# Spreading a weight conversion over three passes and moving low parts to GpSimd

## The chip, the cores and the metric

The kernel runs on one core of a Trainium2 chip. The metric is device time in microseconds (us) of one execution. Engines are named as in the profile: PE is TensorE's matmul, PEld its weight load, DVE is VectorE, ACT ScalarE, POOL GpSimd, SP the engine whose queue issues all the DMAs.

## The reference

A retention layer is followed by two feed-forward layers on 2304 tokens of width 512, all kept in float32:

```
ret = (q @ k^T * scale * decay) @ v              # 4 batches x 8 heads, 576 x 64
x   = (silu(x @ w_gate) * (x @ w_val)) @ w_out   # layer 1, inner width 1536
x   = (max(x @ w_in, 0) ** 2) @ w_out            # layer 2, inner width 2048
```

The activations are float32; the weights of both layers are float64.

## The kernel before, in words

**Stages.** Retention comes first. Then come five passes: (1, 0) and (1, 1) for layer 1, (2, 0), (2, 1) and (2, 2) for layer 2. A pass takes two blocks of tokens (512 each in layer 1, 384 in layer 2) through all "systems" of its layer: a system is 256 inner columns of one weight matrix ("g" gate, "v" value, "i" layer 2's input). There are 12 systems in a pass of layer 1 and 8 in one of layer 2. Pass (1, 0) carries a further 256 tokens, the plain chunk ("c").

**Products.** A system is done as a 2 x 2 block product with seven multiplications instead of eight: `slot(n, i)` does multiplication i of system n into PSUM (`g`, `v`, `z`) and its combinations on ACT and DVE (`cag`, `cav`, `cbg`, `cbv`, 128x512 per row). Each operand is split into a high part (ACT's copy to float32r) and a low part (source minus high, DVE), and PE does three matmuls per product. `hidden` (L678) splits the activated columns: "a" and "b" for the two token blocks, "c" for the plain chunk, into `ho_hi` and `ho_lo`. The second matmul (`out1`, `out2`) adds `oacc` into the resident `xy` on DVE.

**Weights.** A unit is one tile of 64-bit weights: layer 1 has 36 units, layer 2 has 32. `words` (L150) converts a unit in two ACT and four DVE instructions: the clamp (TENSOR_SCALAR on 128x512 f32), a shift and mask (TENSOR_SCALAR on uint32), SCALAR_TENSOR_TENSOR, and a last sum, which the profile calls CUSTOM_DVE_ANT_0 and the order ISA. All write `w`. Two `raw` buffers hold loaded words. Layer 1's results stay in SBUF, at most `HOLD` = 5 at a time; layer 2's are stored in DRAM (`wst`) and loaded again as `w_in` or `wo`. In a layer's first pass POOL forms the combinations of a weight tile (`s`, `w`, `w_in`), ACT and DVE split them into `wi`, and `wi` and `wo` are stored (`win`, `wsp`) for the later passes.

**Order.** The loop at the end emits, for each step n, ten entries of `seq` (slots of system n and n - 1, and the thirds 0, 1, 2 of the output tiles). After each slot it advances the build of the next system's weights and the conversion by `PACE` parts (five parts are a unit). `ensure` (L245) forces a conversion that is needed and not there. A scheduler with its own timeline then orders each engine's queue by when it expects the operands, so that a queue's order is not the emitted order. Each engine works off its queue in order: what stands behind a waiting instruction waits too.

Of the kernel before, what the change touches and what calls it, by code (L numbers as in the profile page):

```python
# [9 lines left out]
F32 = mybir.dt.float32  # L10
F32R = mybir.dt.float32r
U16 = mybir.dt.uint16
U32 = mybir.dt.uint32
AF = mybir.ActivationFunctionType
ALU = mybir.AluOpType
# [6 lines left out]
P = 128  # L22
# [6 lines left out]
M1 = 512  # L29
# [14 lines left out]
UNITS_EARLY = 7  # L44
HOLD = 5

PACE = {(1, 0): 1.3, (1, 1): 1.3, (2, 0): 1.3}

CUT = 256

# [1 line left out]
TINY = float(np.uint32(0x38000000).view(np.float32))  # L52
HUGE = float(np.uint32(0x47F00000).view(np.float32))
# [3 lines left out]
def retention_moe_kernel(  # L57
# [13 lines left out]
    def pool(stack, name, bufs, **kw):  # L71
        return stack.enter_context(
            tc.tile_pool(name=name, bufs=bufs, reuse_waits="tile", **kw)
        )

    keep = pool(ctx, "keep", 1)
    mid = ExitStack()
    ctx.enter_context(mid)
    raw_p = pool(mid, "raw_p", 2)
    cv_p = pool(mid, "cv_p", 1)  # L80
    wb_p = pool(mid, "wb_p", 2)
    part_p = pool(ctx, "part_p", 1, space=bass.MemoryType.DRAM)
    ps_g = pool(ctx, "ps_g", 1, space=PSUM)
# [4 lines left out]
    def f32(ap):  # L88
        return ap.bitcast(F32)
# [3 lines left out]
    class Chained:  # L93


        def __init__(self, engine):
            self.engine, self.last = engine, None

        def __getattr__(self, name):
            op = getattr(self.engine, name)  # L100

            def traced(*args, **kw):
                with ExitStack() as behind:
                    if self.last is not None:
                        behind.enter_context(tc.issue_after(self.last))
                    i = op(*args, **kw)  # L106
                if chain["on"]:
                    self.last = i.ins
                return i

            return traced

    pe, dve, act, pool_e, sp = map(Chained, (nc.tensor, nc.vector, nc.scalar, nc.gpsimd, nc.sync))


    order = [(1, what, f) for k in range(F1 // 2) for what in "gvo" for f in (2 * k, 2 * k + 1)]
    order += [(2, what, f) for k in range(F2 // 2) for what in "io" for f in (2 * k, 2 * k + 1)]
    raw_t, raw_flat, w_t = {}, {}, {}
    spare, ready = [], {}
    loads = {"next": 0, "raw": 0, "open": False, "cap": len(order) - 1, "held": 0}  # L120

    def prefetch(upto):

# [21 lines left out]
    def finish(i):  # L145
        if i in w_t:
            sp.dma_start(out=wst[order[i]], in_=w_t.pop(i).bitcast(F32))
            stored.add(order[i])

    def words(raw, back, flat):  # L150

        ts = dve.tensor_scalar
        both = raw.rearrange("p a (n two) -> p a n two", two=2)
        low, high = both[:, :, :, 0], both[:, :, :, 1]
        low16 = raw.bitcast(U16).rearrange("p a (n four) -> p a n four", four=4)[:, :, :, 1]
        wt = cv_p.tile([P, 512], U32, tag="w", name="w", bufs=HOLD + 1)
        w = wt.rearrange("p (a n) -> p a n", a=2)
        wf = w.bitcast(F32)
        act.activation(out=low, in_=low16, func=AF.Copy, scale=2.0**-13)
        act.activation(out=wf, in_=high.bitcast(F32), func=AF.Abs)  # L160
        yield wt
        ts(out=wf, in0=wf, scalar1=TINY, scalar2=HUGE, op0=ALU.max, op1=ALU.min)
        yield wt
        yield wt
        ts(out=w, in0=w, scalar1=3, scalar2=0x3FFFFFFF, op0=ALU.logical_shift_left, op1=ALU.bitwise_and)
        yield wt
        dve.scalar_tensor_tensor(
            out=w, in0=high, scalar=0xC0000000, in1=w, op0=ALU.bitwise_and, op1=ALU.bitwise_or
        )
        yield wt  # L170
        if back is None:
            adds = [(wt, flat.rearrange("p (n two) -> p n two", two=2)[:, :, 0])]
        else:
            adds = [(w[:, a], low[:, a]) for a in range(2)]
        for to, lo in adds:
            dve.tensor_tensor(out=to, in0=to, in1=lo, op=ALU.add)
# [28 lines left out]
    def catch_up():  # L205
        while behind:
            lo, src, hi = behind.pop(0)
            dve.tensor_tensor(out=lo, in0=src, in1=hi, op=ALU.subtract)

    def split(hi, lo, src):  # L210
        act.copy(hi, src)
        behind.append((lo, src, f32(hi)))
        if not chain["on"]:
            catch_up()
# [51 lines left out]
    def three(dst, a, b, first, last):  # L266
# [5 lines left out]
    tt = dve.tensor_tensor  # L272
# [3 lines left out]
    systems = [  # L276
        (ph, p, k, what)
        for ph, p in passes
        for k in range((F1, F2)[ph - 1] // 2)
        for what in ("gv", "i")[ph - 1]  # L280
    ]
# [26 lines left out]
        split(*xo[i], src)  # L308

    def temp(tag, rows):  # L310
        return c4_p.tile([P, rows, M1], F32, tag=tag, name=f"c{tag}", bufs=1 + (tag[1] == "g"))

    built = {}
    inputs = {}
# [267 lines left out]
    c4_p = pool(ctx, "c4_p", 1, side="right")  # L582
# [93 lines left out]
    hid = {}  # L676

    def hidden(n, which, c):  # L678
        hi = ho_p.tile(list(c.shape), F32R, tag=f"h{which}", name="ho_hi")
        lo = ho_p.tile(list(c.shape), F32R, tag=f"l{which}", name="ho_lo")  # L680
        split(hi, lo, c)
        hid[n, which] = hi, lo

    wos = {}
# [3 lines left out]
    def load_out(n, fs):  # L688
        ph, p = systems[n][:2]
        for f in fs:  # L690
            key = (ph, "o", f)
            w = wos[f] = wo_p.tile([P, 2, 512], F32R, tag="wo", name="wo")
            if p:
                sp.dma_start(out=w.bitcast(F32), in_=wsp[key])
                continue
            if ph == 1:
                ensure(key, ready)
                src = ready.pop(key)
                loads["held"] -= 1
                act.copy(w[:, 0], src)  # L700
                pool_e.tensor_tensor(out=w[:, 1], in0=src, in1=f32(w[:, 0]), op=ALU.subtract)
            else:
                ensure(key, stored)
                sp.dma_start(out=w[:, 1].bitcast(F32), in_=wst[key])
                act.copy(w[:, 0], f32(w[:, 1]))
                tt(out=w[:, 1], in0=f32(w[:, 1]), in1=f32(w[:, 0]), op=ALU.subtract)
            sp.dma_start(out=wsp[key], in_=w.bitcast(F32))

    turn["o"] = 0
# [38 lines left out]
    flip = systems.index((2, 0, 0, "i"))  # L748
# [12 lines left out]
    def after(n, i):  # L761
# [4 lines left out]
        if i in (1, 2, 3, 4, 5, 7):  # L766
            for j in (5, 6) if i == 5 else (i,):
                renew(passes[passes.index(at) + 1], j)

    ho_p = pool(mid, "ho_p", 1)  # L770
    gate_p = pool(mid, "gate_p", 1)
    wo_p = pool(mid, "wo_p", 4)
    pace = {"due": 0.0}
    pumped["limit"] = 10 ** 6
    end = len(systems)
    for n in range(end + 4):
        ph, p, k, what = systems[n] if n < end else (0, None, 0, "")
        tiles = outs.get(n, [])
        cuts = [len(tiles) * x // 3 for x in range(4)] if n != flip + 1 else [0] + 3 * [len(tiles)]
        seq = [(1, n), (7, n - 1), 0, (2, n), (4, n - 1), 1, (6, n), (3, n - 1), 2, (5, n)]  # L780
        if (ph, p) == (1, 0):
            seq.insert(5, (("s", 0), n))
            seq.append((("s", 1), n))
        if n == 0:
            for x in range(4):
                sp.dma_start(out=later[x][0], in_=later[x][1])
            later.clear()
            load_in(1)
            renew((1, 0), 4)
            renew((1, 0), 3)  # L790
        make = build(n + 1) if n + 1 < end else iter(())
        if n + 2 < end and systems[n + 2][1] == 0:
            load_in(n + 2)
        for x in fetch.get(n, []):
            load_out(*x)
        for x in seq:
            if x in (0, 1, 2):
                for fn, *args in tiles[cuts[x]:cuts[x + 1]]:
                    fn(*args)
                continue  # L800
            i, k = x
            if n == flip + 1 and i == 4:
                mid.close()
                ho_p = pool(ctx, "ho2_p", 3)
                wo_p = pool(ctx, "wo2_p", 8)
            if not 0 <= k < end:
                continue
            if isinstance(i, tuple):
                plain_slot(k, i[1])
            else:  # L810
                slot(k, i)
            next(make, None)
            if n < flip - 1:
                pace["due"] += PACE[ph, p]
                pump(int(pace["due"]))
                pace["due"] %= 1
            after(k, i)
        for _ in make:
            pass
        if n == flip - 1:  # L820
            for _ in convert:
                pass

# [60 lines left out]
```

## Time and profile before

| | us |
|---|---|
| median of 3 runs | 903.7 (901.61 to 904.12) |
| the profiled execution | 903.78 |
| its span | 902.0 |
| PE busy | 876.7 |
| DVE busy | 649.2 |
| ACT busy | 397.4 |
| POOL busy | 120.5 |

The span runs from the first to the last instruction; 1.8 us of the profiled execution lie around it. Retention fills the first 98 us; the passes end near 336, 519, 645 and 770 us.

### The profile page before, as it was taken

To read this page: it belongs to the slowest core of one execution; us is meant where nothing else is said; L and a number is where in the kernel's file an instruction comes from. 1 tells how busy PE (TensorE), PEld (TensorE's weight loads), DVE (VectorE), ACT (ScalarE), POOL (GpSimd) and SP (SyncE) were. 2 spreads that over 40 slices of the span, in tenths; PEclk is the share of its full clock that TensorE was granted. 3 is DMA by queue.
4 is the path that set the end of the run, shared out by engine and by line. 5 is a ranking of instruction groups with operands and counts; after the bars stand their busy time and mean duration, and the time that the engine had idled before them with its cause. 6 is when DMAs were issued, how large, how long until landed. Compare 5 with 4: busy or idle time off the path is not lost.

```text
span 902.0 us, 13463 instructions
## 1 busy us (share of the span) xinstructions
PE 876.7 (97%) x5050; PEld 747.6 (83%) x5050; DVE 649.2 (72%) x1019; ACT 397.4 (44%) x708; POOL 120.5 (13%) x131
## 2 busy tenths in 40 slices
PE   8898999999999999999999999999999999999997
PEld 6786778788877778877888889899989889889886
DVE  3889997989898898777747898768543467534443
ACT  2566676654545554544423546544223233233210
POOL 2351522512221110000001231300000000000000
PEclk9999999999999999999999999999999999999999
DMA  9985676656567879889654459855774575666402
GB/s 327 353 297 197 237 265 206 206 206 220 180 216 248 274 276 292 293 291 305 246 180 140 173 205 399 305 188 201 245 243 157 171 224 187 189 219 219 144 34 71
DMA packets 73041, 203.61 MB, mean 226 GB/s; under 512 B 7440, under 2 KB 18192, under 8 KB 72976
## 3 DMA queue, kind: packets, MB, share of 16 engines
q1 hardware_dynamic: 72976, 202.75, 65.7%
q8 instruction: 40, 0.66, 0.3%
q14 instruction: 25, 0.20, 0.1%
HBM read 138.23 MB, written 64.49 MB: 225 GB/s over the span
## 4 chain that ended last, share of the span: by engine, by line
PE 66%; DVE 15%; DMA 11%; issue 4%; ACT 3%; SPq 1%; POOL 1%; ACTq 0%; DVEq 0%; POOLq 0%
PE oacc L106 32%; PE g L106 17%; PE v L106 9%; DMA raw<-in_w 8%; DVE w L106 6%; PE z L106 4%; DVE xy L106 2%; PE o L106 2%; PE s L106 1%; DVE wi L106 1%; ACT w L106 1%; DVE xo_l L106 1%; ACT raw L106 1%; DMA kv_sb<-in_kv 1%; DMA qk_sb<-in_qk 1%
## 5 line engine op out<-in xcount | busy, mean ns | idle before, releaser
L106 PE MATMUL g<-xo_h,wi 128*128 128x384 f32 (+1 forms) x768 | 242.3, 366 | 3.2 <-ACT cbv L106 1.3
L106 PE MATMUL oacc<-wo,ho_hi 128*128 128x512 f32 x576 | 182.4, 392 | 0.2 <-ACT wo L106 0.2
L106 PEld LDWEIGHTS g<-xo_h,wi 128*128 128x128 f32 x768 | 142.4, 188 | 24.5 <-ACT cbv L106 2.9
L106 PE MATMUL oacc<-ho_hi,wo 128*128 128x512 f32 (+1 forms) x480 | 152.1, 372 | 5.1 <-DVE xy L106 3.7
L106 PE MATMUL g<-xo_l,wi 128*128 128x384 f32 (+1 forms) x384 | 139.7, 364 | 0.0
L106 DVE TENSOR_TENSOR xy<-oacc,xy 128x512 f32<-128x512 f32 (+1 forms) x154 | 99.3, 651 | 47.9 <-PE oacc L106 47.5
L106 PE MATMUL v<-xo_h,wi 128*128 128x512 f32 (+1 forms) x384 | 124.7, 365 | 0.1
L106 PEld LDWEIGHTS oacc<-wo,ho_hi 128*128 128x128 f32 x576 | 107.2, 188 | 19.1 <-ACT wo L106 0.6
L106 PE MATMUL oacc<-wo,ho_lo 128*128 128x512 f32 x288 | 113.4, 394 | 0.0
L106 PEld LDWEIGHTS oacc<-ho_hi,wo 128*128 128x128 f32 x480 | 87.9, 188 | 24.1 <-DVE xy L106 5.5
L106 ACT ACTIVATE raw<-raw 128x512 uint32<-128x512 uint16 x68 | 46.0, 677 | 124.8 <-DMA raw<-in_w 112.5
L106 DVE TENSOR_SCALAR w<-w 128x512 f32<-128x512 f32 (+1 forms) x136 | 65.4, 481 | 34.5 <-ACT w L106 33.5
L106 PE MATMUL oacc<-ho_lo,wo 128*128 128x512 f32 (+1 forms) x240 | 89.2, 372 | 0.6 <-DVE ho_lo L106 0.6
L106 DVE TENSOR_TENSOR cbg<-v,cbg 128x384 f32<-128x384 f32 (+1 forms) x72 | 43.0, 598 | 54.1 <-ACT cbg L106 39.7
L106 PEld LDWEIGHTS g<-xo_l,wi 128*128 128x128 f32 x384 | 72.1, 188 | 9.0
L106 PEld LDWEIGHTS v<-xo_h,wi 128*128 128x128 f32 x384 | 71.3, 188 | 9.1 <-DVE cbg L106 0.5
L106 PE MATMUL v<-xo_l,wi 128*128 128x512 f32 (+1 forms) x192 | 69.9, 364 | 0.0
L106 PE MATMUL z<-xo_h,wi 128*128 128x512 f32 (+1 forms) x192 | 62.4, 366 | 1.7 <-DVE cav L106 1.7
L106 PEld LDWEIGHTS oacc<-wo,ho_lo 128*128 128x128 f32 x288 | 54.0, 188 | 11.0
L106 ACT ACTIVATE cag<-g 128x384 f32<-128x384 f32 (+1 forms) x36 | 18.9, 525 | 89.6 <-PE g L106 89.5
L106 ACT CAST ho_hi<-cbg 128x768 fp32r<-128x768 f32 (+1 forms) x36 | 32.6, 906 | 51.5 <-DVE cbg L106 51.5
L106 ACT COPY cbg<-g 128x384 f32<-128x384 f32 (+1 forms) x72 | 37.0, 514 | 39.3 <-PE g L106 39.1
(84 smaller groups left out, 1310.8 us busy)
## 6 DMA issues: line engine op xcount, KB each, us to landing
wi<-win SPq DMA_DIRECT2D x84, 512.0 KB, 4.0
raw<-in_w SPq DMA_DIRECT2D x68, 512.0 KB, 4.4
win<-wi SPq DMA_DIRECT2D x60, 512.0 KB, 3.7
wo<-wsp SPq DMA_DIRECT2D x44, 512.0 KB, 6.0
wsp<-wo SPq DMA_DIRECT2D x28, 512.0 KB, 5.9
qk_sb<-in_qk SPq DMA_DIRECT2D x15, 576.0 KB, 6.9
kv_sb<-in_kv SPq DMA_DIRECT2D x15, 576.0 KB, 6.2
wst<-w SPq DMA_DIRECT2D x32, 256.0 KB, 4.7
```

Of the source, the lines that this page charges most:

```text
L106: i = op(*args, **kw)
```

## The change

- Layer 2's conversion is emitted in all three passes (1, 0), (1, 1) and (2, 0), by new numbers in `PACE` (parts per slot in the first systems of a pass, how many, and parts after that). The buffers `raw_p` and `cv_p` therefore live to the end; half of the `w` buffers (`cv2_p`) and layer 1's intermediates (`c4m_p`) are freed at the switch to layer 2.
- The clamp may not be queued on DVE ahead of the instruction that was the last one two slots earlier (`place`).
- In pass (1, 0), `hidden` computes the low parts of "b" and "c" on POOL instead of DVE. `load_out` does so for layer 2's `wo`.
- In layer 2, "a" has two buffers of `ho_hi` and `ho_lo`, and in steps with "a" tiles the two last of the three tiles come before slot 4 of the system before.

```diff
-PACE = {(1, 0): 1.3, (1, 1): 1.3, (2, 0): 1.3}
+PACE = {(1, 0): (10, 1.5, 1.2), (1, 1): (8, 1.5, 0.1), (2, 0): (8, 1.0, 1.0)}
...
-        wt = cv_p.tile([P, 512], U32, tag="w", name="w", bufs=HOLD + 1)
+        loads["turn"] += 1
+        wt = (cv_p if late2["on"] or loads["turn"] % 2 else cv2_p).tile([P, 512], U32, tag="w", name="w")
...
-        ts(out=wf, in0=wf, scalar1=TINY, scalar2=HUGE, op0=ALU.max, op1=ALU.min)
+        with ExitStack() as held:
+            if place:
+                held.enter_context(tc.issue_after(place[0]))
+            ts(out=wf, in0=wf, scalar1=TINY, scalar2=HUGE, op0=ALU.max, op1=ALU.min)
...
-        split(hi, lo, c)
+        if systems[n][:2] == (1, 0) and which != "a":
+            act.copy(hi, c)
+            pool_e.tensor_tensor(out=lo, in0=c, in1=f32(hi), op=ALU.subtract)
+        else:
+            split(hi, lo, c)
...
-                tt(out=w[:, 1], in0=f32(w[:, 1]), in1=f32(w[:, 0]), op=ALU.subtract)
+                pool_e.tensor_tensor(out=w[:, 1], in0=f32(w[:, 1]), in1=f32(w[:, 0]), op=ALU.subtract)
...
+        if n > flip + 1 and tiles and tiles[0][2] == "a":
+            seq[4:6] = seq[5], seq[4]
+            cuts[2] = 3
...
-            if n < flip - 1:
-                pace["due"] += PACE[ph, p]
+            place[:] = place[1:] + [dve.recent]
+            if (ph, p) in PACE:
+                first, early, later_ = PACE[ph, p]
+                pace["due"] += early if n - systems.index((ph, p, 0, ("gv", "i")[ph - 1][0])) < first else later_
...
-        if n == flip - 1:
+        if (ph, p) == (2, 0) and systems[n + 1][1]:
```

The moves below are at three places. The first is POOL's queue early in pass (1, 0), where `w` and `s` are the weight combinations. Before:

```order
L106 TENSOR_TENSOR s_1503<-w 128x256
L106 TENSOR_TENSOR w<-w 128x256
L106 TENSOR_TENSOR w<-s_1503,w 128x256
L106 TENSOR_TENSOR w<-w 128x256
L106 TENSOR_TENSOR s_1641<-w 128x256
L106 TENSOR_TENSOR w<-w 128x256
L106 TENSOR_TENSOR w<-s_1641,w 128x256
L106 TENSOR_TENSOR w<-w 128x256
L106 TENSOR_TENSOR wo<-w,wo 128x512 x2
L106 TENSOR_TENSOR s_1794<-w 128x256
```

And now, at the same place:

```order
L107 TENSOR_TENSOR ho_lo<-gate,ho_hi 128x512
L107 TENSOR_TENSOR wo<-w,wo 128x512
L107 TENSOR_TENSOR s_1647<-w 128x256
L107 TENSOR_TENSOR w<-w 128x256
L107 TENSOR_TENSOR w<-s_1647,w 128x256
L107 TENSOR_TENSOR w<-w 128x256
L107 TENSOR_TENSOR ho_lo<-cbg,ho_hi 128x1024
L107 TENSOR_TENSOR wo<-w,wo 128x512
L107 TENSOR_TENSOR s_1800<-w 128x256
```

The two low parts of a pair of systems now stand between the weight combinations. The second place is DVE's queue near the end of pass (2, 0), where the weights of its last system are split (`wi` from `w_in` and `s1`). Before:

```order
L106 TENSOR_TENSOR xy_72<-oacc_5892,xy_72 128x4x128
L106 TENSOR_TENSOR ho_lo_5887<-cag_5695,ho_hi_5886 128x768
L106 TENSOR_TENSOR cbg_5696<-v_5814,cbg_5696 128x384
L106 SCALAR_TENSOR_TENSOR cbg_5696<-cbg_5696 128x2x384
L106 TENSOR_TENSOR wi_5929<-w_in_5670,wi_5929 128x512
L106 TENSOR_TENSOR ho_lo_5925<-cbg_5696,ho_hi_5924 128x768
L106 TENSOR_TENSOR xy_72<-oacc_5932,xy_72 128x4x128
L106 TENSOR_TENSOR wi_6023<-s1_5984,wi_6023 128x256
```

Now, from the conversion of that system's second tile (`w_5803`, which becomes `w_in_5790`) on:

```order
L107 ISA w_5803<-raw_5791,w_5803 128x1024
L107 TENSOR_SCALAR w_5814<-w_5814 128x512 x2
L107 SCALAR_TENSOR_TENSOR cag_5822<-g_5821,cag_5822 128x384
L107 SCALAR_TENSOR_TENSOR w_5814<-raw_5801,w_5814 128x512
L107 TENSOR_TENSOR cbg_5823<-v_5950,cbg_5823 128x384
L107 ISA w_5814<-raw_5801,w_5814 128x1024
L107 TENSOR_TENSOR ho_lo_6041<-cag_5822,ho_hi_6040 128x768
L107 SCALAR_TENSOR_TENSOR cbg_5823<-cbg_5823 128x2x384
L107 TENSOR_TENSOR xy_75<-oacc_6086,xy_75 128x4x128
L107 TENSOR_TENSOR ho_lo_6079<-cbg_5823,ho_hi_6078 128x768
L107 TENSOR_TENSOR wi_5991<-w_in_5789,wi_5991 128x512
```

Conversions now stand among the products' combinations there, and the last system's tiles are converted a few instructions before its weights are built. The third place is SP's queue for the same weights. Before:

```order
L106 DMA w_in_5822<-wst_101 128x512
L106 DMA wo_5954<-wst_91 128x512
L106 DMA wo_5959<-wst_92 128x512
L106 DMA wo_5964<-wst_95 128x512
L106 DMA wo_5969<-wst_96 128x512
L106 DMA win_174<-wi_5797 128x1024
L106 DMA w_in_5823<-wst_102 128x512
```

Now:

```order
L107 DMA w_in_5789<-wst_104 128x512
L107 DMA raw_5812<-in_w2 128x1024
L107 DMA wst_105<-w_5803 128x512
L107 DMA wst_106<-w_5814 128x512
L107 DMA wi_6118<-win_156 128x1024
L107 DMA wsp_1373<-wo_6241 128x1024
L107 DMA wsp_1374<-wo_6246 128x1024
L107 DMA w_in_5790<-wst_105 128x512
```

The store and the load of `wst_105` are four queue entries apart; before, the stores of all `wst` lay in the earlier passes.

## Rows read from the trace of the kernel before

**Rows 1.** The page's first line.

```profile
span 902.0 us, 13463 instructions
```

**Rows 2.** By pass: stretch, length, busy PE, PEld, DVE, ACT, POOL, clock, DMA.

```profile
98.00:336.00 238.00, 228.11 (x1149) 189.28 (x1148) 217.93 (x352) 135.92 (x242) 55.52 (x54) 1.00 0.68 232
336.00:519.00 183.00, 181.43 (x806) 147.75 (x805) 137.23 (x215) 81.37 (x131) 9.38 (x10) 1.00 0.71 237
519.00:645.00 126.00, 125.76 (x628) 113.03 (x627) 97.06 (x143) 58.94 (x103) 19.06 (x20) 1.00 0.72 262
645.00:770.00 125.00, 125.00 (x624) 112.47 (x624) 64.83 (x93) 37.55 (x61) 0.00 (x0) 1.00 0.62 198
770.00:902.00 132.00, 127.45 (x624) 112.88 (x622) 56.49 (x81) 28.87 (x48) 0.00 (x0) 1.00 0.44 143
```

**Rows 3.** The same view of parts of passes (1, 0) and (2, 0).

```profile
98.00:198.00 100.00, 93.62 (x477) 77.68 (x476) 92.23 (x149) 62.69 (x117) 29.85 (x30) 1.00 0.68 231
198.00:258.00 60.00, 60.00 (x308) 50.82 (x307) 55.27 (x89) 32.00 (x58) 17.46 (x18) 1.00 0.58 199
258.00:336.00 78.00, 74.49 (x367) 60.77 (x366) 70.43 (x116) 41.23 (x67) 8.20 (x7) 1.00 0.76 260
...
519.00:552.00 33.00, 32.76 (x164) 29.28 (x163) 30.91 (x49) 16.82 (x32) 7.67 (x8) 1.00 0.73 262
```

**Rows 4.** PEld's waits, 98 to 336: total us, times, longest; first and last.

```profile
PEld oacc L106 <- DVE xy L106: 5.5, 7, 1.8
...
PEld v L106 <- DVE cbg L106: 0.3, 1, 0.3
```

**Rows 5.** PEld's waits, 336 to 519, first and last.

```profile
PEld g L106 <- ACT cbv L106: 1.8, 3, 1.2
...
PEld oacc L106 <- ACT ho_hi L106: 0.2, 1, 0.2
```

**Rows 6.** DVE's groups by shape, 98 to 336: busy, mean ns, idle before.

```profile
L106 DVE SCALAR_TENSOR_TENSOR w<-raw,w 128x512 uint32<-128x512 uint32 x39 | 32.0, 821 | 0.4
L106 DVE CUSTOM_DVE_ANT_0 w<-raw,w 128x1024 uint16<-128x1024 uint16 x39 | 29.9, 765 | 0.3
...
L106 DVE TENSOR_TENSOR xy<-oacc,xy 128x512 f32<-128x512 f32 x32 | 21.6, 681 | 0.0
L106 DVE TENSOR_SCALAR w<-w 128x512 uint32<-128x512 uint32 x40 | 20.9, 523 | 0.6
L106 DVE TENSOR_SCALAR w<-w 128x512 f32<-128x512 f32 x40 | 18.4, 461 | 12.1 <-ACT w L106 12.1
...
L106 DVE TENSOR_TENSOR ho_lo<-cbg,ho_hi 128x1024 fp32r<-128x1024 f32 x5 | 6.3, 1263 | 1.0 <-ACT ho_hi L106 1.0
L106 DVE TENSOR_TENSOR ho_lo<-gate,ho_hi 128x512 fp32r<-128x512 f32 x6 | 5.5, 909 | 1.1 <-ACT ho_hi L106 0.9
```

**Rows 7.** The same groups, 336 to 519.

```profile
L106 DVE TENSOR_TENSOR xy<-oacc,xy 128x512 f32<-128x512 f32 x40 | 27.1, 684 | 3.0 <-PE oacc L106 2.8
L106 DVE CUSTOM_DVE_ANT_0 w<-raw,w 128x1024 uint16<-128x1024 uint16 x22 | 15.1, 687 | 0.3
L106 DVE SCALAR_TENSOR_TENSOR w<-raw,w 128x512 uint32<-128x512 uint32 x21 | 14.4, 687 | 0.3
L106 DVE TENSOR_SCALAR w<-w 128x512 f32<-128x512 f32 x20 | 8.5, 426 | 17.5 <-ACT w L106 17.5
...
L106 DVE TENSOR_SCALAR w<-w 128x512 uint32<-128x512 uint32 x20 | 8.4, 422 | 0.3
```

**Rows 8.** DVE's group for layer 2's output weights, 519 to 645.

```profile
L106 DVE TENSOR_TENSOR wo<-wo 128x512 fp32r<-128x512 f32 x16 | 10.6, 685 | 3.2 <-ACT wo L106 3.0
```

**Rows 9.** A low part on POOL, 98 to 336.

```profile
L106 POOL TENSOR_TENSOR wo<-w,wo 128x512 fp32r<-128x512 f32 x10 | 14.5, 1457 | 35.8 <-ACT wo L106 35.8
```

**Rows 10.** DMA issues: count, KB each, median us to landing.

```profile
wst<-w SPq DMA_DIRECT2D x32, 256.0 KB, 4.7
...
w_in<-wst SPq DMA_DIRECT2D x16, 256.0 KB, 5.8
```

More of the change, by code (lines that the diff above doesn't have):

```diff
@@ L76, in retention_moe_kernel @@
     keep = pool(ctx, "keep", 1)
+    raw_p = pool(ctx, "raw_p", 2)
+    cv_p = pool(ctx, "cv_p", 3)
     mid = ExitStack()
     ctx.enter_context(mid)
-    raw_p = pool(mid, "raw_p", 2)
-    cv_p = pool(mid, "cv_p", 1)
+    cv2_p = pool(mid, "cv2_p", HOLD - 2)
     wb_p = pool(mid, "wb_p", 2)
@@ L96, in __init__ @@
         def __init__(self, engine):
-            self.engine, self.last = engine, None
+            self.engine, self.last, self.recent = engine, None, None
         def __getattr__(self, name):
@@ L106, in traced @@
                     i = op(*args, **kw)
+                self.recent = i.ins
                 if chain["on"]:
@@ L119, in retention_moe_kernel @@
     spare, ready = [], {}
-    loads = {"next": 0, "raw": 0, "open": False, "cap": len(order) - 1, "held": 0}
+    loads = {"next": 0, "raw": 0, "open": False, "cap": len(order) - 1, "held": 0, "turn": 0}
+    late2 = {"on": False}
     def prefetch(upto):
@@ L148, in finish @@
             stored.add(order[i])
+    place = []
     def words(raw, back, flat):
@@ L310, in temp @@
     def temp(tag, rows):
-        return c4_p.tile([P, rows, M1], F32, tag=tag, name=f"c{tag}", bufs=1 + (tag[1] == "g"))
+        return (c4_p if tag[1] == "g" else c4m_p).tile([P, rows, M1], F32, tag=tag, name=f"c{tag}", bufs=1 + (tag[1] == "g"))
     built = {}
@@ L678, in hidden @@
     def hidden(n, which, c):
-        hi = ho_p.tile(list(c.shape), F32R, tag=f"h{which}", name="ho_hi")
-        lo = ho_p.tile(list(c.shape), F32R, tag=f"l{which}", name="ho_lo")
-        split(hi, lo, c)
+        kw = dict(bufs=2) if late2["on"] and which == "a" else {}
+        hi = ho_p.tile(list(c.shape), F32R, tag=f"h{which}", name="ho_hi", **kw)
+        lo = ho_p.tile(list(c.shape), F32R, tag=f"l{which}", name="ho_lo", **kw)
+        if systems[n][:2] == (1, 0) and which != "a":
[3 more added lines that the diff above has]
+            split(hi, lo, c)
         hid[n, which] = hi, lo
@@ L768, in after @@
                 renew(passes[passes.index(at) + 1], j)
+    c4m_p = pool(mid, "c4m_p", 1)
     ho_p = pool(mid, "ho_p", 1)
@@ L773, in retention_moe_kernel @@
     pace = {"due": 0.0}
+    place[:] = [dve.last, dve.last]
     pumped["limit"] = 10 ** 6
@@ L803, in retention_moe_kernel @@
                 mid.close()
+                late2["on"] = True
                 ho_p = pool(ctx, "ho2_p", 3)
```

## Prediction

> **What bounds the kernel now.** I read the page's first line [rows 1], then the busy time of every engine by pass, then who PEld waited for, pass by pass. In rows 2 PE is the bound of each pass after retention: 228.1 of 238 us in (1, 0), 181.4 of 183 in (1, 1), 125.8 of 126 in (2, 0), 125.0 of 125 in (2, 1); the 4.6 us in the last row are the end of the kernel. The clock is 1.00 in each row. The matmuls are the same after the change, so it can only win back waits of PE. A PE end is modelled, and a short wait hides in it; PEld, which leads PE, shows more. Its twelve rows in (1, 0), of which rows 4 give the first and the last, add up to 16.4 us, and its nine rows in (1, 1) [rows 5] to 5.5. In (2, 0) PE lost 0.24 us. So some 22 us can be won at most, three quarters of them in (1, 0), where DVE is busy 217.9 of 238 us. Most of those waits are for DVE or ACT results that free a PSUM bank, such as `xy` [rows 4]: DVE works in order, and what frees the bank stands behind a conversion.
>
> DVE's load alone doesn't decide. Rows 3 split the pass: from 198 to 258 DVE is 92% busy and PE loses nothing; from 98 to 198 it is 92% too and PE loses 6.4 us. In (2, 0), from 519 to 552, DVE is 94% busy and PE loses 0.24 us. A wait comes where several DVE instructions that PE doesn't need are queued together, or DVE stands for ACT (12.1 us before the clamp, rows 6).
>
> **Pass (1, 0).** DVE converts 39 units there now [rows 6], 32 after the change, and 22 [rows 7], then 18, in (1, 1); 11 go to (2, 0). The new counts are from the order, between the same combinations. A unit costs DVE 0.821 + 0.765 + 0.523 + 0.461 = 2.57 us in (1, 0) [rows 6], so 7 units are 18.0 us. Twelve low parts leave DVE: six of 128x1024 at 1.263 and six of 128x512 at 0.909 [rows 6], 13.0 us. They become POOL's: 128x512 takes 1.457 us there [rows 9], 128x1024 twice that as an estimate, so 6 x 1.457 + 6 x 2.914 = 26.2 us of POOL.
>
> POOL's work isn't free for DVE. The four conversion rows are slower in (1, 0), with 55.5 us of POOL, than in (1, 1), with 9.4 [rows 2, 6, 7]: 39 x (0.821 - 0.687) + 39 x (0.765 - 0.687) + 40 x (0.523 - 0.422) + 40 x (0.461 - 0.426) = 13.7 us. That is 0.25 us of DVE per us of POOL, and these rows are under half of DVE's work in the pass, so 0.25 is the lower bound; the upper one is 1.0, when DVE stands for the whole POOL instruction. I take 0.35, near the bound that is measured. The 26.2 us then cost DVE 9.2 us, and of the 13.0 us only 3.8 remain. `xy<-oacc`, which reads PSUM, takes 681 ns in one pass and 684 in the other: it pays nothing.
>
> The Trainium skill (SBUF — State Buffer, "Who interferes with whom") says that a VectorE instruction with two SBUF inputs contends with a GpSimd instruction that reads SBUF, and that the later one fully blocks. The trace agrees on which rows pay; by full blocking in every case the 26.2 us would cost DVE 26.2 us and the move of the low parts would be a loss of 13.2.
>
> DVE after: 217.9 - 18.0 - 13.0 + 9.2 = 196.1 us, 0.86 of PE's 228.1 instead of 0.955. What that is worth I bound by two readings. Load: waits were 5.5 us of 183 (3.0%) at 137.2/181.4 = 0.76 and 16.4 of 238 (6.9%) at 0.955; between them 0.86 gives 5.0%, 11.9 us, a gain of 4.5. Bunches: with six units in each pair of systems, where the order before has up to eight, the whole pass could go like 198 to 258 in rows 3, a gain of 16.4. I take 10, the middle. Nothing becomes late on POOL: at 55.5 + 26.2 of 238 us it has room, and `out1` reads these low parts one to two systems (20 to 40 us) later. The POOL row shows what now waits behind a low part: `wo` and the next `s`, both needed a system later.
>
> **Pass (1, 1).** Four units at 0.687 + 0.687 + 0.426 + 0.422 = 2.22 us [rows 7] are 8.9 us of DVE. The longest of the 5.5 us of waits are for ACT's copies, not DVE's [rows 5], so I take 1.5 of them, with 0 and 5.5 as ends.
>
> **Pass (2, 0).** This is what the change pays. DVE gets 11 x 2.22 = 24.4 us of conversion and loses the 10.6 us of `wo` low parts [rows 8], which become 16 x 1.457 = 23.3 us of POOL and cost DVE 0.35 x 23.3 = 8.2. From 97.1 [rows 2] it goes to 119.1 us, 0.947 of PE's 125.8. By load that is like (1, 0) before: 6.7% of 126 us, 8.4 us of waits. By the stretch 519 to 552 [rows 3] it is none. I take the middle, 4.2.
>
> Part of it is a chain with new links. A unit of the last systems now goes through store and reload while the pass runs. From the last sum on `w_5803` to the `wi` that is split from `s1` there are about twenty DVE instructions, some 15 us (an estimate by 0.42 to 0.69 us for a conversion's parts and other 128x512 rows, more for 128x768). The chain needs 4.7 us for the store and 5.8 for the load [rows 10], about 1.5 for the combination on POOL and the split on ACT (an estimate from half of rows 9 and from rows 6), and up to 2.9 more because the load stands in SP's queue behind two `wsp` stores that wait for POOL's low parts (two at 1.457). That is 12.0 to 14.9 us, so the cover is just used up in the last two systems, and in the systems before those it is over 30 us by the same count. Before, all units were stored a pass earlier.
>
> **Costs of nothing.** The place of the clamp adds no instruction; it only lets the products' combinations pass a clamp that waits for ACT. The changed seat of two "a" tiles hands PE the same matmuls; the copy of the next `ho_hi` may now wait for the last tile, but it is needed two systems, 31 us, later, and in (2, 1) DVE is busy 64.8 of 125 us [rows 2]. If that cover fails, it costs a wait of some 0.7 us (one DVE row) in each of twelve steps. Pools that live longer add no instruction. The raw loads, 11 x 512 KB, and their stores go into a pass whose DMA share is 0.72 [rows 2]; in (1, 0), with 0.76 from 258 to 336 [rows 3], loads landed in time for PE, so I give this no price of its own.
>
> **Sum.** -10 - 1.5 + 4.2 = -7.3 us against the profiled execution: its span of 902.0 [rows 1] with 1.8 us around it is 903.8, the same as the median of 903.7. The forecast is **896.5 us**, and its own range, with (1, 0) between -4.5 and -16.4 but not both passes at the same extreme, 890 to 901.
>
> **Rivals.**
> - *No waits at all* (chance 0.10). All of (1, 0) goes like 198 to 258, and (2, 0) like 519 to 552: -16.4 - 1.5 + 0 gives 886. For it: both stretches are over 92% busy. Against: each is short, with few or no conversions in a bunch.
> - *Moved, not removed* (0.22). The waits follow DVE's load: -4.5 in (1, 0), -1.5 in (1, 1), +8.4 in (2, 0) give +2.4; with half of this in doubt, 901 to 906. For it: the load in (2, 0) ends where that of (1, 0) began. Against: rows 3.
> - *POOL stops DVE* (0.16), the slower side. POOL's instructions cost DVE more than 0.35 us each us, since DVE in (2, 0) has little else than rows with two SBUF inputs to do. Without POOL's new work DVE has 97.1 - 10.6 + 24.4 = 110.9 us there, so it passes PE's 125.8 us from a price of 14.9/23.3 = 0.64. At 1.0 it is 134.2 us: +8.4 us, and the reload's chain, with no slack on DVE, adds its 2.9 us. In (1, 0) DVE would have 217.9 - 31.0 + 26.2 = 213.1 us, nearly what it had, a gain of some 2. Together +9: about 912; at 0.7 about 906. For it: the slowed rows. Against: 0.25 measured. The rule of the Trainium skill above (SBUF — State Buffer, "Who interferes with whom") is this case; its full blocking would hold for every instruction, which the measured 0.25 doesn't bear out.
>
> **How the numbers follow.** The forecast has 0.52. The three runs lie within 0.3% of each other, and 0.3% (2.7 us) is about what can be told from no change here. Faster by more, under 901.0: the forecast's 0.52, *no waits* 0.10 and a small part of *moved*, 0.03: 0.65. Slower by more, over 906.4: most of *POOL stops DVE* and the edge of *moved*: 0.15. The rest, 0.20, is the same. The range of 8 in 10 reaches from half of the way to *no waits* to the middle of *moved* and a little further: 889 to 906.
>
> **What would show it.** PEld's waits from 98 to 336 should fall from 16.4 to about 6, and the pass should end some 10 us earlier, with DVE's busy time near 196 and POOL's near 82. `cbg` and `gate` low parts on POOL should take 2.9 and 1.46 us. Pass (2, 0) should be 4 us longer, with DVE near 119 us and waits for `xy`, `wi` or `w`. (2, 1), (2, 2) and the end should take what they took. It is wrong if (2, 0) takes over 135 us (POOL or the reload), if (1, 0) keeps more than 12 us of waits (load decides), or if PE waits for POOL's `ho_lo`.

## The result, and the profile after

The changed kernel takes 909.5 us (median of 6 runs, 907.94 to 910.01), the kernel before 904.0 (901.61 to 905.52) beside it. The ratio is 1.0058 [1.0042, 1.0074]: 5.5 us slower, where 7.2 faster was forecast. The profiled execution took 909.41 us, 1.8 of it around its span:

```profile
span 907.6 us, 13454 instructions
```

The same windows as [rows 2] (length, busy PE, PEld, DVE, ACT, POOL with counts, clock, DMA share, GB/s), of the kernel after:

```profile
98.00:336.00 238.00, 226.33 (x1138) 188.16 (x1138) 201.53 (x310) 128.35 (x227) 74.72 (x65) 0.99 0.58 201
...
519.00:645.00 126.00, 123.82 (x610) 110.79 (x609) 119.82 (x167) 67.49 (x121) 45.06 (x36) 0.99 0.91 325
```

DVE's load moved as meant: 217.9 to 201.5 us in the first window, 97.1 to 119.8 in the third. PE didn't gain by it: it is busy 226.3 us in the first window instead of 228.1. A fixed window holds less work of a slower kernel, so here is the same view by the work, from the first matmul into `z` of (1, 0) to that of (1, 1), before and after:

```profile
88.20:313.10 224.90, 215.25 (x1105) 179.83 (x1104) 205.41 (x331) 132.47 (x241) 59.15 (x55) 1.00 0.65 223
88.30:318.80 230.50, 218.94 (x1123) 183.17 (x1123) 192.70 (x298) 129.46 (x232) 76.70 (x66) 0.99 0.58 202
```

DVE is 12.7 us lighter there, 0.88 of PE's busy time instead of 0.95. PEld's waits in the first fixed window, against the 16.4 us in twelve rows of [rows 4], are in fewer rows and come to 17.9 us:

```profile
PEld oacc L107 <- DVE xy L107: 6.7, 6, 1.9
PEld g L107 <- ACT cbg L107: 4.8, 3, 2.4
PEld oacc L107 <- ACT xy L107: 2.6, 3, 1.2
PEld oacc L107 <- DVE gate L107: 2.0, 2, 1.3
PEld g L107 <- ACT cag L107: 1.3, 1, 1.3
PEld g L107 <- DVE xo_l L107: 0.5, 1, 0.5
```

In (1, 1) the waits fell from 4.9 us to 3.4. (The 5.5 of the prediction hold 0.6 us of waiting for `wo` that belong to (2, 0); the eight rows from 336 to 519, whose first and last are [rows 5], make 4.9.) In (2, 0) they rose from 0.6 to 3.5, most of it in one wait.

DVE's groups of 98 to 336, which answer to [rows 6] (busy, mean ns, idle before):

```profile
L107 DVE SCALAR_TENSOR_TENSOR w<-raw,w 128x512 uint32<-128x512 uint32 x33 | 28.0, 852 | 0.5
L107 DVE CUSTOM_DVE_ANT_0 w<-raw,w 128x1024 uint16<-128x1024 uint16 x32 | 26.4, 826 | 0.2
L107 DVE TENSOR_TENSOR xy<-oacc,xy 128x512 f32<-128x512 f32 x32 | 21.2, 678 | 0.0
L107 DVE TENSOR_SCALAR w<-w 128x512 f32<-128x512 f32 x33 | 18.5, 560 | 9.6 <-ACT w L107 9.6
L107 DVE TENSOR_SCALAR w<-w 128x512 uint32<-128x512 uint32 x33 | 18.3, 558 | 0.4
```

and the low parts on POOL in the same stretch, which [rows 9] stood for:

```profile
L107 POOL TENSOR_TENSOR ho_lo<-cbg,ho_hi 128x1024 fp32r<-128x1024 f32 x5 | 13.4, 2681 | 8.3 <-ACT ho_hi L107 8.3
L107 POOL TENSOR_TENSOR ho_lo<-gate,ho_hi 128x512 fp32r<-128x512 f32 x6 | 9.0, 1499 | 1.5 <-ACT ho_hi L107 1.5
```

Fewer units are converted (32 or 33 instead of 39), but each costs DVE 0.852 + 0.826 + 0.560 + 0.558 = 2.80 us instead of 2.57. Of these rows only `xy<-oacc`, with one input in PSUM, kept its duration (678 ns). The others are longer only where POOL worked beside them. Sorted so over the trace, 25 of the 33 SCALAR_TENSOR_TENSOR rows overlap no POOL instruction and take 0.674 to 0.694 us each; the 8 that overlap one take 1.37 on average. Of the TENSOR_SCALAR rows, 46 alone take 0.42 us and 20 beside POOL 0.88. `xy<-oacc` takes 0.678 us in both cases.

**One wait followed back.** The timeline of the kernel after around PE's longest wait in the pass (start, us, then in brackets the idle time before and what ended it):

```profile
167.61 1.40 DVE L107 TENSOR_SCALAR w<-w 128x512 uint32<-128x512 uint32 x1
168.69 2.58 POOL L107 TENSOR_TENSOR ho_lo<-cbg,ho_hi 128x1024 fp32r<-128x1024 f32 x1
...
169.05 2.77 DVE L107 SCALAR_TENSOR_TENSOR w<-raw,w 128x512 uint32<-128x512 uint32 x1
...
171.86 0.69 DVE L107 CUSTOM_DVE_ANT_0 w<-raw,w 128x1024 uint16<-128x1024 uint16 x1
...
172.58 0.62 ACT L107 CAST wi<-w 128x512 fp32r<-128x512 f32 x1 [2.88 <-DVE w L107]
173.10 0.58 ACT L107 COPY cbg<-g 128x512 f32<-128x512 f32 x1
...
173.74 0.50 PE L107 MATMUL g<-xo_h,wi 128*128 128x512 f32 x1 [2.15 <-ACT cbg L107]
```

Read it from below. PE waits 2.15 us for ACT's copy `cbg`, which frees a PSUM bank. That copy needs only PE's product, but stands on ACT behind a cast that waits 2.88 us for a conversion on DVE. On DVE the SCALAR_TENSOR_TENSOR began 0.36 us after POOL's low part and ended 0.55 us after it: 2.77 us instead of 0.69, the duration that the next conversion row has. No row has PE waiting for POOL's `ho_lo`; it waits for what POOL held up on another engine, through a third.

### The profile page after: what moved, and what is told of

Read it like the earlier page. It is cut to its first block, busy times and chain, and to the rows that moved or that the text cites. A ratio compares the mean times of both kernels' runs of the same rounds, so it can differ in the third digit from the quotient of the medians.

```text
span 907.6 us, 13454 instructions
## 1 busy us (share of the span) xinstructions
PE 878.0 (97%) x5050; PEld 749.8 (83%) x5050; DVE 649.7 (72%) x991; ACT 396.2 (44%) x708; POOL 168.6 (19%) x159
## 4 chain that ended last, share of the span: by engine, by line
PE 60%; DVE 19%; DMA 8%; ACT 4%; issue 4%; POOL 0%; ACTq 0%; SPq 0%; DVEq 0%; POOLq 0%
PE oacc L107 30%; PE g L107 17%; PE v L107 8%; DVE w L107 8%; DMA raw<-in_w 6%; PE z L107 4%; DVE xy L107 3%; DVE xo_l L107 2%; DVE wi L107 1%; DVE cbg L107 1%; ACT w L107 1%; DVE cag L107 1%; ACT raw L107 1%; DVE p_sb L107 1%; DVE ho_lo L107 1%
## 5 line engine op out<-in xcount | busy, mean ns | idle before, releaser
L107 PE MATMUL oacc<-wo,ho_hi 128*128 128x512 f32 x576 | 180.0, 393 | 1.7 <-ACT wo L107 1.7
L107 PE MATMUL v<-xo_h,wi 128*128 128x512 f32 (+1 forms) x384 | 122.8, 365 | 0.3 <-DVE cbg L107 0.3
L107 DVE TENSOR_SCALAR w<-w 128x512 f32<-128x512 f32 (+1 forms) x136 | 72.4, 535 | 27.9 <-ACT w L107 27.1
L107 DVE TENSOR_TENSOR cbg<-v,cbg 128x384 f32<-128x384 f32 (+1 forms) x72 | 42.9, 596 | 39.2 <-ACT cbg L107 22.7
L107 PEld LDWEIGHTS oacc<-wo,ho_lo 128*128 128x128 f32 x288 | 54.3, 189 | 11.2
L107 DVE CUSTOM_DVE_ANT_0 w<-raw,w 128x1024 uint16<-128x1024 uint16 (+1 forms) x70 | 54.8, 785 | 0.7
```

## The experiments

All times are medians of 6 to 12 executions beside the kernel before, which took 902.6 to 904.4 us in these comparisons. The last columns are from the profiles: the time from the first matmul into `z` of (1, 0) to the first of (2, 0) ("layer 1"), and from there to the first of (2, 2) ("layer 2"). What follows, to the last instruction, took 152.1 to 152.8 us everywhere, and what comes ahead 87.4 to 89.4 (92.1 in e14). The forecast was -11.5 us for layer 1 and +4.2 for layer 2. Profiles of kernels that are alike in layer 1 differ by up to 2.9 us there (e1 and e11).

| kernel | us | ratio to before | layer 1 | layer 2 |
|---|---|---|---|---|
| before | 904.0 | 1 | 416.3 | 244.7 |
| after | 909.5 | 1.0058 [1.0042, 1.0074] | 418.4 | 248.3 |
| e1_lows_on_dve | 897.3 | 0.9925 [0.9904, 0.9947] | 407.8 | 247.2 |
| e2_wo_on_dve | 908.1 | 1.0049 [1.0032, 1.0067] | 416.4 | 247.9 |
| e3_spread_alone | 897.1 | 0.9921 [0.9896, 0.9946] | 405.4 | 248.8 |
| e4_lows_alone | 912.7 | 1.0104 [1.0078, 1.0130] | 426.1 | 244.6 |
| e5_halves | 908.9 | 1.0053 [1.0033, 1.0074] | 418.4 | 248.2 |
| e8_spare_sub | 910.8 | 1.0074 [1.0047, 1.0100] | 420.7 | 248.2 |
| e9_spare_set | 902.8 | 0.9987 [0.9967, 1.0007] | 411.8 | 248.4 |
| e10_no_place | 904.1 | 1.0004 [0.9985, 1.0023] | 418.9 | 244.3 |
| e11_no_seats | 898.5 | 0.9939 [0.9916, 0.9962] | 404.9 | 248.1 |
| e12_place_alone | 927.4 | 1.0266 [1.0240, 1.0291] | 407.3 | 276.8 |
| e13_less_pool | 897.2 | 0.9929 [0.9905, 0.9954] | 406.2 | 247.3 |
| e14_spread_over_two | 905.8 | 1.0020 [1.0001, 1.0040] | 406.1 | 256.8 |

**Which part costs it: e1 to e4.** e1 is the kernel after with the low parts of "b" and "c" on DVE again; e2 has only `wo`'s there, e3 both, so that only the spread of the conversion is left. e4 is the kernel before with the low parts of "b" and "c" on POOL.

```diff
 # e1, e3
-        if systems[n][:2] == (1, 0) and which != "a":
-            act.copy(hi, c)
-            pool_e.tensor_tensor(out=lo, in0=c, in1=f32(hi), op=ALU.subtract)
-        else:
-            split(hi, lo, c)
+        split(hi, lo, c)
 # e2, e3
-                pool_e.tensor_tensor(out=w[:, 1], in0=f32(w[:, 1]), in1=f32(w[:, 0]), op=ALU.subtract)
+                tt(out=w[:, 1], in0=f32(w[:, 1]), in1=f32(w[:, 0]), op=ALU.subtract)
```

> The changed kernel with the low parts of b and c back on DVE; all else as changed. Theory 1 (POOL holds DVE): in the changed kernel three of the long waits of PE in (1, 0) (132.1, 173.7, 215.4 us) follow a POOL ho_lo<-cbg of 2.6 to 3.3 us during which a DVE conversion takes 1.7 to 2.8 us instead of 0.7; without it PE's idle time from 98 to 336 falls from 11.7 us to 6 or less, no wait over 2 us is left there and the granted clock stays at 1.00 around it: 901 to 905 us. Theory 2 (the spread itself costs): PE's idle time there stays at 10 to 12 us and the time at 908 to 911.

> The changed kernel with the low parts of layer 2's wo back on DVE; all else as changed. Theory 1 (POOL holds DVE): in (2, 0) DVE's conversion rows come down from 0.77 to 0.96 us to about 0.7, DVE's busy time there stays near 120 us (10.6 us back, some 12 us less of being held), and the wait of 1.7 us for wo at 544.8 goes, with the 3.4 us at half clock behind it: 905 to 908 us. Theory 2 (eleven conversions in (2, 0) are too many for DVE): DVE goes to 125 us or more, (2, 0) gets longer and the time is 910 to 914.

> The changed kernel with both kinds of low parts back on DVE: the conversion's spread, the place of the clamp and the seats of the tiles alone. Theory 1 (POOL holds DVE): the sum of the two runs before, 898 to 903 us, faster than the kernel before. Theory 2 (the spread itself costs): 908 us or more.

> The kernel before with the low parts of b and c of pass (1, 0) on POOL and nothing else changed. Theory 1 (POOL holds DVE): DVE's mean for a conversion's parts in (1, 0) rises as in the changed kernel (0.85, 0.83, 0.56, 0.56 us), PE's idle time from 98 to 336 rises from 9.9 us to 12 or more: 906 to 911 us. Theory 2: the low parts are 11 to 13 us off DVE, PE's idle time falls and the time is 898 to 903.

The spread alone gains 0.8% (e3): layer 1 is 10.9 us shorter and layer 2 4.1 longer. The low parts of "b" and "c" cost 12.2 us in the kernel after (909.5 against e1's 897.3) and 8.3 in the kernel before (912.7 against 904.4 in that comparison). `wo`'s cost nothing that can be told (e2 against after, e1 against e3). e1 and e3 came out 1 to 4 us faster than the lower ends expected by the theory that POOL holds DVE, and e4 1.7 us slower than the upper one. In e2 the wait for `wo` was expected to go, and it stayed (1.8 us, with the half clock behind it), so POOL's low parts of `wo` don't cause it.

In e1 PEld waits 6.5 us from 98 to 336:

```profile
PEld oacc L107 <- DVE xy L107: 4.5, 4, 1.9
PEld oacc L107 <- ACT xy L107: 1.0, 1, 1.0
PEld g L107 <- ACT cbg L107: 1.0, 1, 1.0
```

That is about a third of the kernel after. Here is e1's fixed window, and behind it the same work as in the kernel after (first matmul into `z` of (1, 0) to that of (1, 1), 1123 or 1124 matmuls):

```profile
98.00:336.00 238.00, 233.16 (x1192) 197.04 (x1191) 206.26 (x338) 133.54 (x233) 50.29 (x54) 1.00 0.61 214
...
88.80:308.30 219.50, 214.66 (x1124) 182.55 (x1123) 187.50 (x308) 130.02 (x232) 54.02 (x56) 1.00 0.61 212
```

Over the same work DVE is busy 187.5 us in e1 and 192.7 in the kernel after, although the latter has handed its low parts to POOL. A unit takes DVE 2.43 us in e1:

```profile
L107 DVE SCALAR_TENSOR_TENSOR w<-raw,w 128x512 uint32<-128x512 uint32 x35 | 25.7, 740 | 0.3
L107 DVE CUSTOM_DVE_ANT_0 w<-raw,w 128x1024 uint16<-128x1024 uint16 x34 | 24.9, 732 | 0.3
L107 DVE TENSOR_SCALAR w<-w 128x512 f32<-128x512 f32 x35 | 17.2, 493 | 3.9 <-ACT w L107 3.9
L107 DVE TENSOR_SCALAR w<-w 128x512 uint32<-128x512 uint32 x35 | 16.3, 469 | 0.3
```

**Late results or held instructions: e8, e9, e5.** POOL's low parts end later than DVE's would. e8 takes that away: it is e1 (the real low parts on DVE) and has POOL compute the same subtraction once more into a tile that nothing reads. In e9 POOL instead clears the source tile, after its last use, twice. e5 is the kernel after with POOL's instruction cut in two rows.

```diff
 # e8, added behind split(hi, lo, c) in pass (1, 0), "b" and "c"
+            d = dum_p.tile([P, 2, M1], F32R, tag="d", name="dum")[:, :, :c.shape[-1]]
+            pool_e.tensor_tensor(out=d, in0=c, in1=f32(hi), op=ALU.subtract)
 # e9, at the same place
+            for _ in range(2):
+                pool_e.memset(c, 0.0)
 # e5
-            pool_e.tensor_tensor(out=lo, in0=c, in1=f32(hi), op=ALU.subtract)
+            for r in range(2):
+                pool_e.tensor_tensor(out=lo[:, r], in0=c[:, r], in1=f32(hi)[:, r], op=ALU.subtract)
```

> The first experiment's kernel (low parts on DVE) and, beside them, twelve spare subtractions on POOL of the same size on the same operands, into a tile that nothing reads. No result comes from POOL later than before. Theory 1 (POOL holds DVE): about as slow as the changed kernel or slower, since DVE has the low parts too: 906 to 914 us, with a conversion's parts at a mean of 0.55 to 0.85 us in (1, 0). Theory 3 (the low parts come late from POOL, and PE or ACT wait for that): nothing waits for the spare ones, 897 to 899 us.

> As the spare subtractions, but each is two POOL memsets of the dead source tile, which write SBUF and read nothing. Theory 1 in its form that the shared thing is the path by which POOL reads SBUF and by which DVE reads its second operand: no slowing, 896 to 900 us, however long POOL is busy. Theory 1 in the form that any POOL work slows DVE: slower by the same measure per us of POOL as the spare subtractions, 902 us or more.

> The changed kernel with each low part on POOL cut into its two rows: twice as many instructions of half the length (about 1.3 and 0.75 us), the same elements. If the length of one hold is what matters (a DVE instruction stands until one POOL instruction ends), the waits of PE over 1 us in (1, 0) get fewer and the half clock goes: 902 to 906 us. If the sum of POOL's time matters, it stays at 908 to 911 us.

e8 is as slow as the kernel after (910.8), 13.5 us over e1, though no instruction waits for what POOL was given. Its window, the same by the work, and POOL's new group:

```profile
98.00:336.00 238.00, 226.34 (x1138) 187.79 (x1137) 209.35 (x320) 127.44 (x225) 75.89 (x65) 0.99 0.58 199
...
88.70:319.20 230.50, 219.22 (x1124) 183.28 (x1123) 200.52 (x308) 129.17 (x232) 77.44 (x66) 0.99 0.58 202
```

```profile
L107 POOL TENSOR_TENSOR dum<-cbg,ho_hi 128x1024 fp32r<-128x1024 f32 x5 | 16.3, 3267 | 6.7 <-ACT ho_hi L107 6.7
```

PE's 226.3 us and POOL's 75.9 are nearly those of the kernel after (226.3 and 74.7). Nor does POOL hold the tiles that it reads for too long: no wait of ACT or DVE in the window names its spare instruction. ACT's waits for POOL's weight combinations, which stand behind it in the queue, are 7.4 us, against 6.1 in e1 and 5.3 in the kernel after. So it is POOL's work beside DVE that costs, not the lateness of its result. e5 is no better than the kernel after: the halves take 1.59 and 1.04 us on POOL where the whole took 2.68 and 1.50, and two shorter holds cost what one costs. e9 falls between the two readings that were put up for it. It puts 17.5 us of writes on POOL (67.8 us in the window against 50.3) and costs 5.5 us. Its groups of the first window:

```profile
L107 DVE SCALAR_TENSOR_TENSOR w<-raw,w 128x512 uint32<-128x512 uint32 x33 | 23.2, 709 | 0.3
L107 DVE TENSOR_SCALAR w<-w 128x512 uint32<-128x512 uint32 x33 | 19.6, 599 | 0.3
L107 POOL MEMSET cbg<- 128x1024 f32 x10 | 10.5, 1046 | 11.6 <-DVE ho_lo L107 11.3
L107 POOL MEMSET gate<- 128x512 f32 x12 | 7.4, 614 | 11.0 <-DVE ho_lo L107 10.6
```

The row with two SBUF inputs isn't slower than in e1 (709 against 740 ns), TENSOR_SCALAR is (599 against 469). Per us that POOL's busy time in the window rises over e1, the subtraction costs the kernel 13.5/25.6 = 0.53 us (e8), the memset 5.5/17.5 = 0.31.

**What moves the conversions: e10, e12, e11.** e10 is e1 without the clamp's `place`; e12 is the kernel before with `place` alone; e11 is e1 without the changed seats.

```diff
 # e10
-            if place:
+            if place and False:
 # e12, against before
+            if place:
+                held.enter_context(tc.issue_after(place[0]))
...
+            place[:] = place[1:] + [dve.recent]
 # e11
-        if n > flip + 1 and tiles and tiles[0][2] == "a":
-            seq[4:6] = seq[5], seq[4]
-            cuts[2] = 3
```

> The first experiment's kernel without the place of the clamp: the conversion's new numbers and the rest remain. If the gain of the spread comes from the place (a clamp that waits for ACT no longer stands ahead of the combinations), it goes back to 902 to 906 us and DVE's wait for ACT's w in (1, 0) is 12 us or more. If it comes from fewer conversions in (1, 0), it stays at 896 to 899 us.

> The kernel before with the place of the clamp and nothing else of the change: the old pace numbers, the conversion ends with pass (1, 1), no low parts on POOL. By the order it converts 32 units in (1, 0) as the changed kernel does, 24 in (1, 1) and hardly any after. If the place is what the spread's gain comes from, it is 895 to 900 us, and (2, 0) stays without waits. If the pace numbers and (2, 0) are needed too, (1, 1) takes the waits: 901 to 906 us.

> The first experiment's kernel without the changed seats of the two a tiles in layer 2: a check that this edit costs nothing, as the prediction says. 896 to 899 us, the same as the first experiment; a cost or gain of more than 2 us would show as waits of PE after 519 us.

Without `place` the new `PACE` does nothing (904.1 us): the scheduler takes the conversions forward again, 38 of them into (1, 0) and none into (2, 0), and DVE stands before the clamp for 17.0 us, as it did for 12.1 in [rows 6]:

```profile
L107 DVE TENSOR_SCALAR w<-w 128x512 f32<-128x512 f32 x38 | 19.2, 505 | 17.0 <-ACT w L107 17.0
```

`place` alone missed both of its readings. It gives layer 1 its 9 us, but the last eight units, where hardly any were expected, then end behind the first matmul into `z` of (2, 0). There PE waits 22.0 us at once (total, times, longest):

```profile
PE oacc L106 <- ACT ho_hi L106: 22.0, 1, 22.0
```

My reading, which no further run tests: before the change `raw` and `w` share memory that layer 2 gets only when the conversion has ended, so the longer-lived pools belong to the spread. The seats cost and give nothing (898.5 against 897.3, the intervals overlap).

**Could it be better: e13, e14.** e13 is e3 with layer 1's `wo` low parts on DVE too; e14 is e3 with a faster pace in (1, 1), so that only 4 units are left for (2, 0).

```diff
 # e13
-                pool_e.tensor_tensor(out=w[:, 1], in0=src, in1=f32(w[:, 0]), op=ALU.subtract)
+                tt(out=w[:, 1], in0=src, in1=f32(w[:, 0]), op=ALU.subtract)
 # e14
-PACE = {(1, 0): (10, 1.5, 1.2), (1, 1): (8, 1.5, 0.1), (2, 0): (8, 1.0, 1.0)}
+PACE = {(1, 0): (10, 1.5, 1.2), (1, 1): (12, 1.5, 1.5), (2, 0): (8, 1.0, 1.0)}
```

> The third experiment's kernel (both low parts on DVE) with the low parts of layer 1's wo moved from POOL to DVE as well: POOL loses some 15 us in (1, 0), DVE gains 12 instructions of some 0.7 us. By theory 1 (0.6 us of DVE per us of POOL) that is even on DVE's busy time, 8.4 us against 9, with shorter holds of DVE: 895 to 898 us. If DVE's load decides, the same. If it were better to have more on POOL, 899 or more.

> The third experiment's kernel (both low parts on DVE) with pace 1.5 in all of pass (1, 1): by the order 25 units are converted in (1, 1) instead of 18, and four in (2, 0) instead of eleven. The run of the clamp's place alone had 24 units in (1, 1) without a wait of PE there, so if (2, 0)'s waits (3.5 to 5 us in the first and third experiment) come from the eleven units, it gains 2 to 4 us: 893 to 896 us. If they come from the switch of the pools and the first loads of wo, it stays at 896 to 899.

e13 is even with e3: POOL has 36.3 us in the window instead of 51.8, and DVE the work. e14 missed: its layer 2 took 256.8 us, with two new waits of PE in (2, 0), each with half clock behind it:

```profile
PE g L107 <- DVE cag L107: 3.2, 1, 3.2
PE g L107 <- ACT cag L107: 2.2, 1, 2.2
```

What these two wait for isn't settled. (The profiled execution of e14 took 908.9 us, 3.1 over the median.) e1, e3 and e13 are the fastest, some 897.2 us, ahead of both kernels.

## Why the prediction was wrong

**The step that failed** is "(1, 0): -10", and in it the price of POOL's work: "I take 0.35, near the bound that is measured." I took POOL's work for an average load on DVE, so much per us, put it into DVE's busy time, and read PE's waits from that. Two things were wrong.

- *The size.* The conversion rows alone show 33 x 0.112 + 32 x 0.094 + 33 x 0.067 + 33 x 0.089 = 11.9 us more in the kernel after than in e1's durations, for 74.7 - 50.3 = 24.4 us more of POOL: 0.49, without DVE's other rows. With all rows, over the same work: the kernel after has 22.7 us more of POOL than e1 and is rid of 11.2 us of low parts on DVE (the two groups below), and yet DVE is busy 5.2 us longer: 16.4/22.7 = 0.72. e8 against e1 gives 13.0/23.4 = 0.56. In (2, 0), from e2 (window row below) to after, DVE gains 119.8 - 114.6 us and is rid of the 10.6 of [rows 8], for 23.6 us of POOL: 15.8/23.6 = 0.67.

```profile
L107 DVE TENSOR_TENSOR ho_lo<-cbg,ho_hi 128x1024 fp32r<-128x1024 f32 x5 | 7.3, 1466 | 1.6 <-ACT ho_hi L107 1.6
L107 DVE TENSOR_TENSOR ho_lo<-gate,ho_hi 128x512 fp32r<-128x512 f32 x5 | 3.9, 785 | 6.8 <-ACT ho_hi L107 6.8
...
519.00:645.00 126.00, 124.12 (x610) 110.63 (x609) 114.61 (x182) 67.42 (x118) 21.47 (x20) 0.99 0.87 320
```

- *The way it counts.* Over (1, 0) DVE's busy time still fell by 12.7 us and the waits didn't. What POOL adds isn't spread over DVE's queue, but stands in it as single holds of up to 2.1 us, with ACT and PE behind them, as in the timeline above. My load reading (0.955 to 0.86) would have a gain at any price under 1. The kernel after and e3 refute it: by the work, DVE's share of PE's busy time is 0.88 in both (e3's row below), and from 98 to 336 PEld waits 17.9 us in one and 5.5 in the other.

```profile
88.30:306.70 218.40, 214.59 (x1124) 182.56 (x1124) 188.11 (x311) 130.96 (x233) 54.47 (x56) 1.00 0.61 213
```

My sign "(1, 0) keeps more than 12 us of waits (load decides)" came true, but not for the reason in its brackets. "Nothing becomes late on POOL" was right, and beside the point: I looked for PE waiting for POOL's result (no row has that, and e8 has no such result), not for POOL in DVE's way.

The rival *POOL stops DVE* had the mechanism and, at 906 to 912, the time. But it put the loss into (2, 0), from a price of 0.64, and left a gain of 2 us in (1, 0). The price was passed in (2, 0), but DVE is 119.8 of 126 us busy there, and e2, without POOL's new work in (2, 0), loses 3.2 us in layer 2 where the kernel after loses 3.6; (1, 0) decided. The Trainium skill (SBUF — State Buffer, "Who interferes with whom") says the engine that comes second blocks fully; the trace agrees for a single pair (2.77 us beside 2.58 of POOL), and 0.56 to 0.72 over a pass is less since DVE, I take it, at times runs a row that doesn't contend, or none. I set the rule aside because of an average of 0.25 from [rows 6, 7], in which the rows that met no POOL instruction hide those that did: before the change, too, 28 SCALAR_TENSOR_TENSOR rows of [rows 6] ran alone at 0.685 us and 11 beside POOL at 1.16. And "the trace agrees on which rows pay" was half right: the two TENSOR_SCALAR rows among the four have one SBUF input, which the rule as I gave it doesn't cover.

**What held, and what was luck.** With both sets of low parts on DVE (e3) the sum is as forecast, 897.1 us (896.5). Layer 1 is at -10.9 us (forecast -11.5; e1 and e11, which differ from it in layer 2 alone, have -8.5 and -11.4). PEld's waits in (1, 0) come to 5.5 in e3 and 6.5 in e1 ("about 6"). So the -10 was a size for the spread with POOL left alone, and *Bunches* was nearer to it than load. In the kernel after, (1, 1) gave 1.5 us of waits (1.5).

Layer 2's +4.1 in e3 (+4.2) is luck. I had it from DVE's load and from a chain through `xy`, `wi` or `w`; in the runs it is one wait for `wo`, 1.9 us of PE, and 1.7 us of work lost at half clock behind it. In e1, whose profiled execution has a wait of 1.5 us there and no half clock behind it, layer 2 loses 2.5. ACT's copy of `wo` stands there for the load from `wst`, in the kernel after and in e3:

```profile
544.15 0.62 ACT L107 CAST wo<-wo 128x512 fp32r<-128x512 f32 x1 [1.36 <-DMA wo<-wst]
...
531.54 0.62 ACT L107 CAST wo<-wo 128x512 fp32r<-128x512 f32 x1 [1.27 <-DMA wo<-wst]
```

The transfers of (2, 0) are the term that I gave "no price of its own", from a stretch with a DMA share of 0.76; here the share is 0.91. What makes this load late, the traffic or its place in SP's queue, no run tests. DVE's 119.8 us in (2, 0) (119.1) is luck as well: the conversions cost what I had (24.8 us in e2, forecast 24.4) and POOL's work more, but the window holds 610 matmuls instead of 628, and less of DVE's other work.

**What I gave too little weight.** I listed the clamp's place among the costs of nothing and put the gain down to the new pace. By e10 and e12 the place is what moves the conversions out of (1, 0); the pace alone does nothing.

**The rest of the 5.5 us.** PEld's waits rose by 2.9 us in all (21.9 to 24.8), the time by 5.5. In the profiled execution 3.4 us of PE's work were lost at half clock, behind two waits of PE; one is in the next section. How much of the 5.5 that is stays open, since the clock differs from one execution to the next, and in e1 it doesn't order their times: its six had a mean granted clock of 0.991 to 1.000, and the one at 0.991 took 896.9 us, the one at 1.000 took 897.6.

## What to carry to other kernels

An elementwise instruction moved to GpSimd isn't gone from VectorE: price it as a hold, of up to its own length, on whatever contending VectorE row meets it (here those with two SBUF inputs and TENSOR_SCALAR, 0.56 to 0.72 us per us of GpSimd in all), and ask who stands behind that row, on ScalarE too. Test the move with a spare copy of the instruction whose result nobody reads, as e8 does: it shows the price before any dependence does. And don't read PE's waits from another engine's busy share: at the same 0.88 of VectorE they were 5.5 us in one kernel here and 17.9 in another. Compare such shares over the same work, since a fixed window holds less of a slower kernel.

## What the runs showed of the hardware

**Half clock behind a wait.** The 2.15 us wait in the timeline above cost more than itself in that execution. PE alone, in windows of 1 us (busy PE, granted clock behind it), kernel after:

```profile
174.00:175.00 1.00, 1.00 (x5) 0.91 0.74 262
175.00:176.00 1.00, 1.00 (x5) 0.50 0.89 352
176.00:177.00 1.00, 1.00 (x6) 0.50 0.96 344
177.00:178.00 1.00, 1.00 (x4) 0.50 0.95 242
178.00:179.00 1.00, 1.00 (x5) 0.88 0.70 283
```

The clock was at 0.50, its lower level of 1.2 GHz, for over 3 us once PE was working again: 0.09 + 3 x 0.50 + 0.12 = 1.7 us of work lost. The same came after a 1.72 us wait for `wo` near 544. It came after a wait of 1.31 us in e11, too. But e4 had a wait of 2.99 us and kept its clock:

```profile
177.00:178.00 1.00, 0.00 (x0) 1.00 0.98 401
178.00:179.00 1.00, 0.07 (x1) 1.00 0.87 356
179.00:180.00 1.00, 1.00 (x5) 1.00 0.70 119
```

So the length of the wait alone doesn't decide; what does stays open.

**Writes alone hold DVE too.** The memsets of e9 read nothing, and still its TENSOR_SCALAR rows on uint32 are 28% longer than e1's. Sorted over e9's trace from 98 to 336, the 13 TENSOR_SCALAR rows of the conversions that ran beside a memset and no other POOL instruction take 0.69 us on average and the 40 that ran beside nothing 0.42; the three conversion rows with two SBUF inputs that ran beside a memset alone take 0.68 to 0.69, as they do undisturbed. The Trainium skill (SBUF — State Buffer, "Who interferes with whom") has it that a GpSimd instruction that only writes doesn't contend with a two-input VectorE row, while `tensor_scalar` can take the shared pair of ports; e9's 709 and 599 ns agree with both. Which mode these rows run in no run here shows.
